# Two paddings in SBUF that shift where the tiles of a convolution and feed-forward kernel begin

## The chip, the cores and the metric

The kernel runs on one core of a Trainium2 chip. The metric is device time in microseconds (us), from three runs of the kernel before: 1163.24, 1163.75 and 1163.84 us, median 1163.75 us. Smaller is better. The engines are named as the profile names them: PE (TensorE's matmuls), PEld (its weight loads), DVE (VectorE), ACT (ScalarE), POOL (GpSimd) and SP (the engine that issues nearly all DMAs).

## The reference

Two layers follow each other. The first is a causal convolution over 7 positions whose weights are given for each token and head, through a softmax; the second is a feed-forward layer with an ELU between its two products.

```python
# x: (4, 4096, 192), weight_gen: (4, 4096, 8 heads, 7 taps)
w = softmax(weight_gen)                       # over the 7 taps
out = einsum('bshk,bskhg->bshg', w, x_unf)    # 7 shifted rows of x, 24 columns per head
# tokens 16384, w_in (192, 2048), w_out (2048, 192)
h = out.reshape(16384, 192) @ w_in
g = where(h > 0, h, exp(min(h, 0)) - 1)       # ELU
return g @ w_out
```

## The kernel before

The 16384 tokens are cut into 32 chunks (`blk`, NB) of 512 tokens, and the 2048 hidden columns into 16 slices (NF), taken two at a time as 8 pairs (`k`, NP). One chunk and one pair make a step `s`: 256 steps. In a step PE forms the two slices' h in PSUM (`product_in`, L685), ACT and DVE make ELU's two parts of them in SBUF (`elu`, L742 to L754), and two steps later PE adds their product with w_out to the sums in PSUM (`product_out`, L713). The convolution of a chunk is made well ahead, nearly all of it on POOL (L508 and L524), and DVE and ACT turn its result into x's parts (`split`, L629 to L639); DMAs on SP's queue then copy parts between the upper and lower 64 partitions (L657).

Precision decides how the operands look. From the second chunk on, each factor is split into a high part, rounded to the type fp32r, and a low part, the rest. So x becomes `xhi` and `xlo`, ELU's value becomes `hi` and `lo` (two rings of seven tiles of 512 columns), w_in becomes `WI` with a high and a low half, and w_out becomes `WO`, whose row holds the high 192 columns and behind them the low 192. h is the sum of three products (xhi with both halves of WI, xlo with the high half) over three pieces of 64 rows: nine matmuls of 512 columns in each half of the partitions. The sum over w_out has a matmul of 384 columns with `hi` as stationary operand (both halves of WO in one go) and one of 192 with `lo`. Only the first chunk (`plain`) uses whole fp32 operands, which take two passes each. Every matmul uses 64 rows of the array, and the upper and lower 64 partitions work side by side: matmuls stand in pairs in the program.

In L685 the stationary operand (loaded on PEld) is a piece of WI and the moving operand is a piece of xhi or xlo. In L713 the stationary operand is a piece of hi or lo, and the moving one a row of WO.

A planner (`Plan`) orders all of it before anything is issued: each task has an engine, a cost from a formula (`pe`, `act`, `dve`, `pool`, `dma`) and a due time, tasks are placed into the earliest gap, and a table (NUDGE) moves some due times. Tiles come from rings (`ring`): the n-th use of a ring waits for the users of the tile that lies `bufs` uses back. No cost, due time or wait depends on an address.

Where a tile lies follows from the order of first use: each tile is placed behind the one before, at a multiple of 32 bytes. The constants come first (`ident`, `scratch`, `WI`, `WO`), then the rings of the pool `sb`. `scratch` is one number per partition, used once to load ACT's table (L885, L886). `wm` holds the largest of the seven weights for each token and head: DVE writes it in L469 and reads it in L471.

Of the kernel before, what the change touches and what calls it, by code (L numbers as in the profile page):

```python
# [10 lines left out]
F32 = mybir.dt.float32  # L11
# [41 lines left out]
class Plan:  # L53
# [13 lines left out]
    def add(self, engine, cost, run, reads=(), writes=(), due=None, port=False):  # L67
        t = Task(engine, cost, run, due, port or engine == "pool")
        for h in reads:
            t.needs.update(h.writers)  # L70
        for h in writes:
            t.needs.update(h.users)
            if not h.users:
                if h.make:
                    t.makes.append(h)
                if h.before:
                    t.needs.update(h.before.users)
        for h in (*reads, *writes):
            h.users.append(t)
        for h in writes:  # L80
            h.writers.append(t)
        t.needs.discard(t)
        t.at = len(self.tasks)
        self.tasks.append(t)
        return t
# [50 lines left out]
def conv_elu_kernel(  # L136
# [12 lines left out]
    P, T, HK = weight_gen.shape  # L149
# [7 lines left out]
    H = HK // K // Q  # L157
# [5 lines left out]
    J = N // (A * S)  # L163
# [38 lines left out]
    def rows(ap, t0, n):  # L202

        return ap.rearrange("(a r) t d -> r a t d", r=R)[t0 // T][:, t0 % T:t0 % T + n]

    def quadrants():

        return [(slice((s * Q + q) * A, (s * Q + q + 1) * A), s, q)
                for s in range(S) for q in range(Q)]

    const = ctx.enter_context(tc.tile_pool(name="const", bufs=1))
# [1 line left out]
    ps = ctx.enter_context(tc.tile_pool(name="ps", bufs=1, space=bass.MemoryType.PSUM))  # L213

    ident = const.tile([P, P], F32, name="ident")
    scratch = const.tile([P, 1], F32, name="scratch")

# [11 lines left out]
    def ring(name, shape, bufs, dtype=F32, pool=sb):  # L231
        return Ring(pool, shape, dtype, name, bufs)
# [4 lines left out]
    r_m_out = ring("m_out", [P, 2, D], 5, I32)  # L237
    r_xw = ring("xw", [P, HALO + J, DQ], 3)
    r_wg = ring("wg", [P, J, H, K], 3)
    r_wm = ring("wm", [P, J, H, 1], 1)  # L240
    r_ws = ring("ws", [P, J, H, 1], 1)
    r_pa = ring("pa", [P, J, H, G], 2)
    r_pb = ring("pb", [P, J, H, G], 1)
# [26 lines left out]
    def act(cols, psum=False):  # L270
        return cols / 1.2 + (70 if psum else 110)

    def dve(cols):
        return cols / 0.96 + 70
# [9 lines left out]
    def dma(packets, byts):  # L284
        return packets * max(9 + byts / 12, 22) / 20
# [7 lines left out]
    def due1(k):  # L293
        if k < len(FIRST):
            return T0 + FIRST[k]
        return T0 + FIRST[-1] + (k - len(FIRST) + 1) * STEP
# [131 lines left out]
    def chunk(blk):  # L428

        n, t0 = J, blk * J * S  # L430
        xw, wg, wm, ws = r_xw.new(), r_wg.new(), r_wm.new(), r_ws.new()
        wg_h[blk] = wg
        xw_h[blk] = xw
        k, kk = n * H, n * H * K

        def w():
            return wg.t[:, 0:n]

        def wide(h):
            return h.t.to_broadcast([P, n, H, K])  # L440

        def load(to, src, n, d, at=0, both=False, only=quadrants()):
            def run():
                for p, s, q in only:
                    eng = nc.scalar if both and q else nc.sync
                    eng.dma_start(out=to()[p], in_=rows(src, t0 + s * J + at, n)[  # L446
                        :, :, q * d:(q + 1) * d])
            return run

        def load_w(only=quadrants()):  # L450
            return load(lambda: w().rearrange("p t h k -> p t (h k)"), weight_gen, n, H * K,
                        both=blk == 0, only=only)

        if blk == 0:
            add("dma", 700 + Q * S * ISSUE // 2, load_w(), writes=[wg], due=-2)
        for one in quadrants() if blk else ():
            add("dma", max(dma(A * n, H * K * 4), ISSUE), load_w([one]), writes=[wg])
        if blk == 0:
            xw_h[blk] = xw = [xw, Handle()]
            m = n + HALO  # L460
            for i, (a, b) in enumerate(((0, m - JH), (m - JH, m))):
                add("dma", dma(P * (b - a), DQ * 4),
                    load(lambda a=a, b=b: xw[0].t[:, a:b], x, b - a, DQ, a),
                    writes=[xw[i]], due=-1 + i)
        else:
            for one in quadrants():
                add("dma", max(dma(A * (n + HALO), DQ * 4), ISSUE),
                    load(lambda: xw.t, x, n + HALO, DQ, only=[one]), writes=[xw])
        add("dve", dve(kk), lambda: nc.vector.tensor_reduce(  # L469
            out=wm.t[:, :, :, 0], in_=w(), axis=AX.X, op=ALU.max), reads=[wg], writes=[wm])  # L470
        add("dve", dve(kk), lambda: nc.vector.tensor_tensor(  # L471
            out=w(), in0=w(), in1=wide(wm), op=ALU.subtract), reads=[wm], writes=[wg], port=True)
        add("act", act(kk), lambda: nc.scalar.activation(
            out=w(), in_=w(), func=ACTF.Exp), writes=[wg])
        add("dve", dve(kk), lambda: nc.vector.tensor_reduce(
            out=ws.t[:, :, :, 0], in_=w(), axis=AX.X, op=ALU.add), reads=[wg], writes=[ws])
        add("act", act(k), lambda: nc.scalar.activation(
            out=ws.t, in_=ws.t, func=ACTF.Copy, bias=1e-9), writes=[ws])
        add("dve", 6.4 * k + 60, lambda: nc.vector.reciprocal(out=ws.t, in_=ws.t),
            writes=[ws])  # L480
        if blk == 0:
            wb_h[blk] = [r_h.new(), r_h.new()]
            for i, h in enumerate(wb_h[blk]):
                def half(t, i=i):
                    return t[:, i * JH:(i + 1) * JH]

                def bank(h=h):
                    return h.t[:, 0:kk // 2].rearrange("p (t h k) -> p t h k", h=H, k=K)

                add("dve", dve(kk // 2), lambda half=half, bank=bank: nc.vector.tensor_tensor(  # L490
                    out=bank(), in0=half(w()), in1=half(wide(ws)), op=ALU.mult),
                    reads=[ws, wg], writes=[h], port=True, due=due1(0) - 14000 + 1000 * i)
                if OWN[blk][i] < K:
                    add("act", act(kk // 2, True), lambda half=half, bank=bank: nc.scalar.copy(
                        out=half(w()), in_=bank()), reads=[h], writes=[wg])
            return
        add("dve", dve(kk), lambda: nc.vector.tensor_tensor(  # L497
            out=w(), in0=w(), in1=wide(ws), op=ALU.mult), reads=[ws], writes=[wg], port=True)
# [384 lines left out]
    with tc.manual_schedule():  # L883

        nc.vector.memset(scratch, 0.0)  # L885
        add("act", 1500, lambda: nc.scalar.activation(out=scratch, in_=scratch, func=ACTF.Exp),  # L886
            due=2500)
        make_identity(nc, ident)
        turn_over(14)
        for s in range(len(todo) + LAG):  # L890
            now = todo[s] if s < len(todo) else None
            up = todo[s - LAG] if s >= LAG else None
            if now:
                blk, k = now
                if k == 0:
                    chunk(blk)
                    if blk < 2:
                        summed(blk, s, OWN[blk])
                    else:
                        conv(blk, s)  # L900
                if blk == 0:
                    if k in in_pieces:
                        weights_in(k, in_pieces[k])
                    weights_out(k)
            period(s, now, up)
            if up and up[1] == NP - 1:
                drain(up[0], s)
        plan.issue()
# [34 lines left out]
```

## Time and profile before

| what | value |
|---|---|
| median of three runs | 1163.75 us |
| runs | 1163.24 to 1163.84 us |
| profiled execution, first to last instruction (span) | 1161.3 us |
| median less span | 2.45 us |
| PE busy | 1154.9 us, 99% of the span |
| PEld, ACT, DVE, POOL busy | 90%, 79%, 73%, 60% |
| share of PE in the chain that ended last | 98% |

The profiled execution has no time of its own beside the span; what lies around it is taken as the difference to the median. Matmuls overlap in the records (a pair starts before the one ahead of it has ended): a busy PE says little, and the distance from one start to the next is what tells the pace.

### The profile page before, as it was taken

To read this page: it belongs to the slowest core of one execution; us is meant where nothing else is said; L and a number is where in the kernel's file an instruction comes from. 1 tells how busy PE (TensorE), PEld (TensorE's weight loads), DVE (VectorE), ACT (ScalarE), POOL (GpSimd) and SP (SyncE) were. 2 spreads that over 40 slices of the span, in tenths; PEclk is the share of its full clock that TensorE was granted. 3 is DMA by queue.
4 is the path that set the end of the run, shared out by engine and by line. 5 is a ranking of instruction groups with operands and counts; after the bars stand their busy time and mean duration, and the time that the engine had idled before them with its cause. 6 is when DMAs were issued, how large, how long until landed. Compare 5 with 4: busy or idle time off the path is not lost.

```text
span 1161.3 us, 32341 instructions
## 1 busy us (share of the span) xinstructions
PE 1154.9 (99%) x12844; PEld 1048.7 (90%) x12844; DVE 847.7 (73%) x1502; ACT 913.7 (79%) x1794; POOL 698.3 (60%) x424
## 2 busy tenths in 40 slices
PE   9999999999999999999999999999999999999998
PEld 6699999999989989989999998998999999999997
DVE  7977768776767777777776677776777776777664
ACT  6778778787778878777878777887777887787775
POOL 4666874846687777865557755567755567653000
PEclk9999999999999999999999999999999999999999
DMA  8831322331233232213332223331223321111100
GB/s 194 165 69 43 65 65 67 71 70 43 57 66 74 49 79 54 59 43 69 70 70 49 47 46 70 71 70 40 53 49 70 70 65 35 26 31 42 42 16 15
DMA packets 143127, 71.04 MB, mean 61 GB/s; under 512 B 98816, under 2 KB 141824, under 8 KB 142976
## 3 DMA queue, kind: packets, MB, share of 16 engines
q1 hardware_dynamic: 142112, 68.72, 27.0%
q8 instruction: 101, 1.65, 0.6%
q14 instruction: 50, 0.41, 0.1%
q10 hardware_dynamic: 864, 0.25, 0.1%
HBM read 31.98 MB, written 12.58 MB: 38 GB/s over the span
## 4 chain that ended last, share of the span: by engine, by line
PE 98%; SPq 1%; DMA 0%; ACT 0%; issue 0%; DVE 0%; DVEq 0%; ACTq 0%
PE h L685 46%; PE accd L713 25%; PE acc L713 25%; PE accd L566 0%; PE acc L566 0%; SPq L446 0%; DMA raw_in<-in_moe_w_in 0%; SPq L369 0%; PE h L681 0%; ACT xhi L646 0%; DVE raw_out L867 0%; ACT acc L329 0%; ACT raw_in L332 0%; SPq L404 0%; ACT raw_out L861 0%
## 5 line engine op out<-in xcount | busy, mean ns | idle before, releaser
L747 DVE SCALAR_TENSOR_TENSOR h<-e,h 128x512 f32<-128x512 f32 x496 | 321.8, 693 | 279.8 <-ACT e L744 278.9
L742 ACT ACTIVATE e<-h 128x512 f32<-128x512 f32 x512 | 280.4, 600 | 171.5 <-PE h L685 171.3
L685 PE MATMUL h<-xhi,WI 64*128 64x512 f32 x2976 | 392.5, 394 | 0.0
L754 DVE TENSOR_TENSOR lo<-h,hi 128x512 fp32r<-128x512 f32 x496 | 326.4, 688 | 14.5 <-ACT hi L752 0.7
L752 ACT CAST hi<-h 128x512 fp32r<-128x512 f32 x496 | 290.7, 587 | 53.9 <-DVE h L747 41.2
L685 PEld LDWEIGHTS h<-xhi,WI 64*128 64x128 f32 x2976 | 279.1, 185 | 48.5
L713 PE MATMUL accd<-WO,hi 64*128 64x384 f32 x1984 | 305.9, 357 | 0.0
L713 PE MATMUL acc<-WO,hi 64*128 64x384 f32 x1984 | 304.6, 355 | 0.0
L524 POOL TENSOR_TENSOR pa<-pa,pb 128x768 f32<-128x768 f32 x150 | 289.9, 1932 | 17.0 <-DVE pb L508 5.5
L744 ACT ACTIVATE e<-e 128x512 f32<-128x512 f32 x512 | 297.9, 637 | 0.9
L508 POOL TENSOR_TENSOR pb<-xw,wg 128x768 f32<-128x768 f32 (+1 forms) x179 | 278.0, 1553 | 11.7
L713 PE MATMUL acc<-WO,lo 64*128 64x192 f32 x1984 | 255.6, 249 | 0.0
L713 PE MATMUL accd<-WO,lo 64*128 64x192 f32 x1984 | 254.8, 248 | 0.0
L508 POOL TENSOR_TENSOR pa<-xw,wg 128x768 f32<-128x768 f32 (+1 forms) x31 | 47.2, 1524 | 305.3 <-DVE wg L497 289.3
L685 PE MATMUL h<-xlo,WI 64*128 64x512 f32 x1488 | 214.6, 390 | 0.0
L713 PEld LDWEIGHTS acc<-WO,lo 64*128 64x128 f32 x1984 | 198.5, 187 | 4.6
L713 PEld LDWEIGHTS acc<-WO,hi 64*128 64x128 f32 x1984 | 196.3, 185 | 4.8
L713 PEld LDWEIGHTS accd<-WO,lo 64*128 64x128 f32 x1984 | 198.8, 188 | 0.1
L713 PEld LDWEIGHTS accd<-WO,hi 64*128 64x128 f32 x1984 | 195.1, 184 | 0.1
L685 PEld LDWEIGHTS h<-xlo,WI 64*128 64x128 f32 x1488 | 144.5, 184 | 28.2
L524 POOL TENSOR_TENSOR xc<-pa,pb 128x768 f32<-128x768 f32 x30 | 55.5, 1851 | 2.4
L639 DVE TENSOR_TENSOR xlo<-xt,xhi 128x768 fp32r<-128x768 f32 (+1 forms) x32 | 37.9, 1184 | 1.0
(84 smaller groups left out, 487.1 us busy)
## 6 DMA issues: line engine op xcount, KB each, us to landing
xw<-in_x SPq DMA_DIRECT2D x124, 168.0 KB, 3.5
xhi<-xhi SPq DMA_DIRECT2D x62, 192.0 KB, 3.0
xlo<-xlo SPq DMA_DIRECT2D x62, 192.0 KB, 2.9
out_dram<-raw_out SPq DMA_DIRECT2D x124, 96.0 KB, 1.9
wg<-in_weight_gen SPq DMA_DIRECT2D x126, 28.0 KB, 2.2
raw_out<-in_moe_w_out SPq DMA_DIRECT2D x8, 384.0 KB, 6.2
raw_in<-in_moe_w_in SPq DMA_DIRECT2D x12, 192.0 KB, 5.3
raw_in<-in_moe_w_in SPq DMA_DIRECT2D x8, 96.0 KB, 2.9
```

Source lines behind the costliest of these rows:

```text
L508: lambda: eng.tensor_tensor(out=h.t[:, 0:J], in0=xw.t[:, j0 + k:j0 + k + J, :].rearrange("p j (h g) -> p j h g", g=G), in1=wg.t[:, j0:j0 + ...
L524: add("pool", pool(J * DQ), lambda b=b, to=to: nc.gpsimd.tensor_tensor(out=to.t, in0=a.t, in1=b.t, op=ALU.add), reads=[b] if to is a else ...
L639: add("dve", dve(C * n * A), lambda i=i: nc.vector.tensor_tensor(out=to(xlo, i), in0=xt(i), in1=to(xhi, i).bitcast(F32), op=ALU.subtract), ...
L685: return lambda: nc.tensor.matmul(out=h.t, lhsT=w_in_f[k][1]()[p, c] if w is None else WI[p, k, w, c], rhs=x.t[p, c, c0:c0 + 2].rearrange( ...
L713: return nc.tensor.matmul(out=to(), lhsT=src.t[p, g * P:(g + 1) * P], rhs=w, start=start, stop=False, skip_group_check=True).ins
L742: add("act", act(N, True), lambda: nc.scalar.activation(out=e.t, in_=h.t, func=ACTF.Relu, scale=-1.0), reads=[h], writes=[e])
L744: add("act", act(N), lambda: nc.scalar.activation(out=e.t, in_=e.t, func=ACTF.Exp, scale=-1.0), writes=[e])
L747: add("dve", dve(N), lambda: nc.vector.scalar_tensor_tensor(out=to.t, in0=e.t, scalar=-1.0, in1=h.t, op0=ALU.add, op1=ALU.max), reads=[e, ...
L752: add("act", act(N, True), lambda: nc.scalar.copy(out=hi.t, in_=h.t), reads=[h], writes=[hi])
L754: add("dve", dve(N), lambda: nc.vector.tensor_tensor(out=lo.t, in0=h.t, in1=hi.t.bitcast(F32), op=ALU.subtract), reads=[h, hi], writes=[lo])
```

## The change

Two tiles that hold few bytes are made larger. `scratch` is allocated with 32 numbers per partition in place of one, and the kernel uses the first; `wm` is allocated with twice its rows, and the kernel uses the first half. Nothing is read or written that was not before, and every engine's instructions and waits stand in the same order with the same shapes.

```diff
-    scratch = const.tile([P, 1], F32, name="scratch")
+    scratch = const.tile([P, 32], F32, name="scratch")[:, 0:1]
...
-    r_wm = ring("wm", [P, J, H, 1], 1)
+    r_wm = ring("wm", [P, 2 * J, H, 1], 1)
...
-        xw, wg, wm, ws = r_xw.new(), r_wg.new(), r_wm.new(), r_ws.new()
+        xw, wg, wm, ws = r_xw.new(), r_wg.new(), r_wm.new(lambda t: t[:, 0:J]), r_ws.new()
```

What moves is the start of each tile behind them. In bytes within a partition (for a ring, its first tile):

```
tile      before   mod 256   mod 64     after    mod 256   mod 64
ident      16512     128        0        16512     128        0
scratch    17024     128        0        17024     128        0
WI         17056     160       32        17152       0        0
WO         41632     160       32        41728       0        0
wg         66208     160       32        66304       0        0
xw         68896      32       32        68992     128        0
wm         85024      32       32        85120     128        0
ws         85152     160       32        85376     128        0
raw_in     85280      32       32        85504       0        0
pa        123680      32       32       123904       0        0
xhi       132896      32       32       133120       0        0
e         160544      32       32       160768       0        0
hi        174368      32       32       174592       0        0
xlo       191776      32       32       192000       0        0
lo        210208      32       32       210432       0        0
xc        224544      32       32       224768       0        0
```

All tiles from WI on began at 32 above a multiple of 64, and begin at a multiple of 64 now. The pieces that a matmul reads lie at multiples of 512 bytes (WI, hi, lo), 1024 (xhi, xlo) or 1536 (WO) from their tile's start, so they share its remainder. WI and WO lay 128 bytes apart from xhi, xlo, hi and lo modulo 256, and lie at the same remainder now.

## Rows read from the trace of the kernel before

**Rows 1.** The page: busy us of each engine, share of the span, instructions.
```profile
PE 1154.9 (99%) x12844; PEld 1048.7 (90%) x12844; DVE 847.7 (73%) x1502; ACT 913.7 (79%) x1794; POOL 698.3 (60%) x424
```

**Rows 2.** The page: chain that ended last, by engine.
```profile
PE 98%; SPq 1%; DMA 0%; ACT 0%; issue 0%; DVE 0%; DVEq 0%; ACTq 0%
```

**Rows 3.** Chain in order of time, steady part: start us, us, what.
```profile
142.29 4.21 PE h L685 x36
151.07 4.21 PE h L685 x36
159.85 4.21 PE h L685 x36
...
1143.39 4.21 PE h L685 x36
```

**Rows 4.** Windows of 8.78 us: busy us of engines, clock, DMA share, GB/s.
```profile
140.00:148.78 8.78, 8.78 (x103) 8.78 (x102) 7.53 (x16) 7.95 (x19) 2.65 (x2) 1.00 0.41 81
148.78:157.56 8.78, 8.78 (x103) 8.78 (x102) 6.71 (x11) 7.23 (x15) 7.99 (x5) 1.00 0.53 125
1000.00:1008.78 8.78, 8.78 (x104) 7.99 (x102) 5.22 (x9) 6.50 (x13) 8.39 (x6) 1.00 0.01 2
```

**Rows 5.** Groups of instructions, PE: shapes, count, busy us, mean ns, idle before.
```profile
L685 PE MATMUL h<-xhi,WI 64*128 64x512 f32 x2976 | 392.5, 394 | 0.0
L713 PE MATMUL accd<-WO,hi 64*128 64x384 f32 x1984 | 305.9, 357 | 0.0
L713 PE MATMUL acc<-WO,hi 64*128 64x384 f32 x1984 | 304.6, 355 | 0.0
L685 PE MATMUL h<-xlo,WI 64*128 64x512 f32 x1488 | 214.6, 390 | 0.0
```

**Rows 6.** Timeline of PE, one step's matmuls and the next stage.
```profile
319.94 1.56 PE L685 MATMUL h<-xhi,WI 64*128 64x512 f32 x12
321.34 0.86 PE L685 MATMUL h<-xlo,WI 64*128 64x512 f32 x6
322.03 0.34 PE L713 MATMUL acc<-WO,hi 64*128 64x384 f32 x2
322.21 0.25 PE L713 MATMUL acc<-WO,lo 64*128 64x192 f32 x2
322.30 0.36 PE L713 MATMUL acc<-WO,hi 64*128 64x384 f32 x2
322.50 0.25 PE L713 MATMUL acc<-WO,lo 64*128 64x192 f32 x2
322.58 0.37 PE L713 MATMUL acc<-WO,hi 64*128 64x384 f32 x2
```

**Rows 7.** Timeline of PEld in the same stage.
```profile
322.21 0.19 PEld L713 LDWEIGHTS acc<-WO,hi 64*128 64x128 f32 x2
322.32 0.19 PEld L713 LDWEIGHTS acc<-WO,lo 64*128 64x128 f32 x2
322.50 0.19 PEld L713 LDWEIGHTS acc<-WO,hi 64*128 64x128 f32 x2
```

**Rows 8.** Chain in the first chunk, with whole fp32 operands.
```profile
32.10 2.58 PE h L685 x12
34.68 0.16 PE accd L713
```

**Rows 9.** Weight loads of two lines: duration ns min/median/max, first and last start.
```profile
L566 PEld LDWEIGHTS acc<-v,ident x28: 186/190/190, 7.3 to 39.9; 128*128 128x128 f32 x28
...
L685 PEld LDWEIGHTS h<-xhi,WI x2976: 183/185/189, 61.0 to 1146.3; 64*128 64x128 f32 x199
```

**Rows 10.** Chain in the prologue: start us, us, what.
```profile
9.41 3.78 DMA raw_in<-in_moe_w_in
13.18 0.02 issue
...
15.49 2.98 PE h L681 x24
```

**Rows 11.** The same DMAs, issue to landing.
```profile
DMA to landing us min/median/max: 2.3/4.4/7.5
```

**Rows 12.** POOL's additions of the convolution: duration ns min/median/max.
```profile
L524 POOL TENSOR_TENSOR pa<-pa,pb x150: 1820/1852/2670, 58.2 to 1048.5; 128x768 f32<-128x768 f32 x150
```

## The prediction

> **What bounds the kernel now.** I read the busy line first: PE is busy for 99% of the span, ACT for 79%, DVE for 73% [rows 1]. A busy PE alone proves little, so the second view is the chain that ended last: 98% of it is PE's own work, with 1% of SP's issue at the start [rows 2]. The third is that chain in order of time. The reader is to see how regular it is: from 142.29 us to 1143.39 us the same stretch of 36 matmuls of L685 returns, and 1001.10 us are 114 times 8.78 us to within 0.2 us [rows 3]. The fourth is a table of windows of just that length. In three of them POOL's work goes from 2.65 to 8.39 us, DVE's from 7.53 to 5.22 and the share of the DMA engines from 0.53 to 0.01, at a granted clock of 1.00 (2.4 GHz) [rows 4], and the period stays 8.78 us. So PE waits for nobody there, and nobody's traffic in SBUF slows it. What the change can do to the time is what it does to PE's own reading of its operands, and next to nothing else.
>
> The pace inside a period: nine pairs of matmuls of 512 columns, from 319.94 to 322.03 us, are 2.09 us, or 232 ns a pair [rows 6]. In L713 one round of `hi` (384 columns) and `lo` (192) takes from 322.30 to 322.58, 0.28 to 0.29 us, 288 ns when the period is divided: (8.78 - 18 x 0.232) / 16 [rows 3, 6]. Counts: 2976 + 1488 matmuls of L685 are 2232 pairs, and 1984 + 1984 of `hi` are 1984 rounds [rows 5]. 2232 x 0.232 = 518 us and 1984 x 0.288 = 571 us: 1089 of the 1161.3 us, and the rest is prologue, first chunk and the last sums.
>
> **The change part by part.** It adds, removes and moves no instruction, wait or DMA on any queue. It alters start addresses, so each term is the difference in how long the same instruction takes.
>
> 1. *L685's matmuls.* 512 columns at one per cycle of 2.4 GHz would be 213 ns; a pair takes 232, 19 more. The trace has one neighbour: with whole fp32 operands in the first chunk 12 matmuls, six pairs, take 2.58 us, 430 ns a pair [rows 8], which is two cycles per column (426.7) and 3 ns. xhi began 32 bytes above a multiple of 64 there as well. So a shifted start costs nothing when a column has two cycles, and 16 ns remain that show only at one column per cycle. Nothing in this trace says whether these 16 ns come from the start address or belong to reading 4 bytes per cycle: no operand of that kind begins elsewhere. Bounds: below, all 16 ns go, 2232 x 0.0156 = 35 us less; above, a collision of the two operands, which the third case prices at as much again, 35 us more. Value taken: 0, as for the nearest row, the fp32 pass, where the same start costs nothing that can be seen.
>
> 2. *L713's rounds.* The loads for `lo` start 0.11 us after those for `hi`, and the matmuls with `lo` start 0.18 us after that, with which the next loads for `hi` start [rows 7, 6]: a round is one load of 128 columns and one stream of 384. The load can be compared: L566 loads `ident`, which begins at a multiple of 128 in both kernels, in 190 ns, and L685 loads WI, shifted by 32, in 185 [rows 9]. The start does not lengthen a load, so that part gets 0. The stream of 384 takes 0.18 us against 160 ns at 2.4 GHz. Of the 20 ns, 3 are again the fixed part; 10 to 17 could go or double: 20 to 33 us either way over 1984 rounds. Value taken: 0, for the reason of point 1.
>
> 3. *ACT, DVE and POOL.* They too read and write at new starts. Whatever it does to them stands beside PE's stream: ACT, the fullest, works 7.95 of 8.78 us in the fullest of the three windows [rows 4], so it would have to become 10% slower before PE waits. 0.
>
> 4. *DMAs.* The only one in the chain is w_in's load, 3.78 us of it, before PE's first product at 15.49 us [rows 10]. Landings of its kind lie between 2.3 and 7.5 us [rows 11], so -1.5 to +3.7 us are the bounds; the bytes and the source rows in HBM are as before, and I take 0. All later DMAs have PE's period as cover.
>
> The sum against the profiled execution is 1161.3 + 0, and with the 2.45 us around it 1163.7 us.
>
> Here the Trainium skill speaks against a gain: SBUF — State Buffer, Specifications (TRN2), gives lines of 16 bytes and a penalty for each step to a new line. Every start was a multiple of 32 already, so by that rule no operand touches one line more or less, and the sum stays 1163.7; the equal weight loads agree, and no row shows the lines themselves.
>
> **The rivals.**
>
> *The shift is what costs PE its 16 ns (faster).* For it: the excess appears only where a column has a single cycle, it grows with the columns (19 ns on 512, while from `lo`'s start to the next `hi`, over 192 columns, it is 0.08 to 0.09 us against 80 ns [rows 6]), and all operands of this kind share the one odd start. A stall for each block of 64 bytes would look like this. Against it: a contiguous stream that starts shifted touches 33 blocks of 64 bytes in place of 32, which is 3% at most, not 7%; and loads don't mind. Price: L685 gives 35 us and L713 at least 20, together 55: 1109 us. If only half of the excess is due to the start, 1136. ACT's 7.95 us would then stand against a period of some 8.4, so not every block would gain in full.
>
> The Trainium skill has a figure for this rival: TensorE: Matmul & The Clock Gate, Back-to-back issue gap, gives N/2.4 + 2.5 ns between matmuls, 215.7 ns for 512 columns. By it 16 ns of 232 are no part of the stream, and without them in L685 alone the time would be 1128 us as an estimate; the fp32 rows agree with such a fixed part (3 ns), and the page doesn't tie it to an address.
>
> *Both of PE's reads fall in step (slower).* WI and WO lay 128 bytes apart from the operands that they meet, modulo 256, and now lie at the same remainder. If PE's weight load and its stream meet in the same part of SBUF, they wait for each other during each load, 0.11 of every 232 ns. For it: two engines can slow each other here, as POOL's additions do, with 1852 ns in the median and 2670 at worst [rows 12]. Against it: the two read at different speeds, so their phase slides through all remainders anyway, and no other reader ever disturbed PE's 8.78 us [rows 3, 4]. It decides from about 1 ns a pair (2.3 us over 2232 pairs). Price: one more excess of the present size in L685, 35 us, 1199 us; at POOL's worst ratio, 44% on each load's 0.11 us, it would be 48 ns a pair and 1271.
>
> *The prologue alone moves.* w_in's first load lands earlier or later within its bounds: 1162.2 to 1167.4 us. The first is within what can be told from no change (2.3 us, 0.2%), the second is just beyond.
>
> **How the numbers follow.** No change: 0.50, and its own range is 1161.4 to 1166.1. The shift costs PE its excess: 0.37, with times from 1109 to 1160. In step: 0.11. The prologue by itself beyond 0.2%: 0.02, slower. About 0.2% is what a measurement of this kernel can tell from no change. So faster 0.37, same 0.50, slower 0.13. The range goes from 1108, the full price of the faster rival, to 1167.4, the prologue's worst: outside lie the slower rival and a gain beyond 55 us, together under 2 in 10.
>
> **What would show it.** If I am right, the period stays 8.78 us, nine pairs 2.09 us and a round 288 ns, and the span differs by under 2 us, at the start. If nine pairs take 1.94 to 2.0 us, the faster rival holds for L685, and a shorter step from `hi` to `lo` shows it for L713. If only L685 or only L713 becomes longer, the reads are in step there. A changed period with unchanged distances inside the two stages would mean a wait that I have not seen, and all of this would be wrong.

## The result, and the profile after

1150.81 us in the median of 4 runs (1150.17 to 1152.1), against 1163.8 us of before beside it: ratio 0.9891, 95% interval 0.9877 to 0.9905. The kernel became 1.1% faster. The time lies inside the forecast range; the likeliest case, no change, did not come about, and the period, forecast to stay at 8.78 us, became 8.67.

The page of the kernel after: busy time of each engine, and the chain that ended last by engine.
```profile
PE 1141.7 (99%) x12844; PEld 1039.1 (90%) x12844; DVE 852.0 (74%) x1502; ACT 912.2 (79%) x1794; POOL 697.9 (61%) x424
...
PE 96%; SPq 1%; ACT 1%; DVE 1%; issue 0%; DMA 0%; DVEq 0%; ACTq 0%
```
PE is still busy for 99% and still holds the chain, now 96% of it where it had 98% [rows 1, 2]. The span is 1149.1 us, 12.2 less than in the profiled execution of before.

The chain of the kernel after, in order of time: start us, us, what.
```profile
306.63 4.15 PE h L685 x36
310.77 1.11 PE acc L713 x16
311.89 1.14 PE accd L713 x16
313.02 1.14 PE acc L713 x16
314.16 1.14 PE accd L713 x16
315.30 4.15 PE h L685 x36
...
323.97 4.15 PE h L685 x36
...
349.99 4.15 PE h L685 x36
```
The period was 8.78 us [rows 3]; it is (349.99 - 306.63) / 5 = 8.67 us now, with nobody but PE in it. PE does the same 36 + 64 matmuls in 0.11 us less.

The timeline of PE in the same kernel, one whole period: start us, us, instruction.
```profile
332.48 1.57 PE L685 MATMUL h<-xhi,WI 64*128 64x512 f32 x12
333.89 0.86 PE L685 MATMUL h<-xlo,WI 64*128 64x512 f32 x6
334.59 1.53 PE L685 MATMUL h<-xhi,WI 64*128 64x512 f32 x12
335.95 0.84 PE L685 MATMUL h<-xlo,WI 64*128 64x512 f32 x6
336.63 0.34 PE L713 MATMUL acc<-WO,hi 64*128 64x384 f32 x2
336.80 0.25 PE L713 MATMUL acc<-WO,lo 64*128 64x192 f32 x2
336.89 0.36 PE L713 MATMUL acc<-WO,hi 64*128 64x384 f32 x2
...
341.16 1.57 PE L685 MATMUL h<-xhi,WI 64*128 64x512 f32 x12
```
The second nine pairs take 336.63 - 334.59 = 2.04 us; before they took 2.09 [rows 6]. Sixteen rounds of L713 take 341.16 - 336.63 = 4.53 us. Medians over all steady periods (from start to start of the matmul records, between 150 and 1120 us): the block of L685, its 18 pairs, went from 4206 to 4147 ns, and that of L713, its 16 rounds, from 4574 to 4526. That is 3.3 ns a pair and 3.0 ns a round. Over 124 periods (2232 pairs / 18) it is 7.3 + 6.0 = 13.3 us, more than the 12.2 that the span lost.

The two profiled executions differ in two more places. First, in the prologue of the kernel after (chain):
```profile
9.90 3.70 DMA raw_in<-in_moe_w_in
...
15.96 2.98 PE h L681 x24
18.94 2.58 PE h L685 x12
```
The first product starts 0.47 us later than in [rows 10], and the fp32 pairs take the same 2.58 us as in [rows 8]. Second, in waits. The chain of the kernel after around 666 us:
```profile
664.57 0.33 SPq L876
...
666.38 1.80 SPq L446
...
668.75 0.02 SPq L700
...
668.81 1.39 PE acc L713 x16
```
PE reaches this L713 while SP's queue still issues DMAs (L876, L446), behind which stands the no-op of L700 that L713 waits for. This period lasts 9.11 us. After has three periods more than 60 ns too long, by 0.96 us together; before had two, by 0.26. So 13.3 - 0.5 - 0.7 = 12.1 us, the span's loss to within 0.1. Neither difference is shown to come from the change. Over all the runs below the first product starts between 15.42 and 16.28 us, and e1, e2 and e3, whose pace is nearly that of before, have 0.87 to 1.08 us of such long periods, with waits for L700 as well (in e3 three, 0.8 us together).

The weight loads, duration ns min/median/max:
```profile
L713 PEld LDWEIGHTS accd<-WO,hi x1984: 183/184/185, 76.1 to 1144.1; 64*128 64x128 f32 x199
```
A load's own record is as long as L685's in [rows 9]; only the step from one instruction to the next became shorter.

### The profile page after: what moved, and what is told of

It is laid out like the page before. It is cut to its first block, busy times and chain, and to the rows that moved or that the text cites. A ratio compares the mean times of both kernels' runs of the same rounds, so it can differ in the third digit from the quotient of the medians.

```text
span 1149.1 us, 32341 instructions
## 1 busy us (share of the span) xinstructions
PE 1141.7 (99%) x12844; PEld 1039.1 (90%) x12844; DVE 852.0 (74%) x1502; ACT 912.2 (79%) x1794; POOL 697.9 (61%) x424
## 4 chain that ended last, share of the span: by engine, by line
PE 96%; SPq 1%; ACT 1%; DVE 1%; issue 0%; DMA 0%; DVEq 0%; ACTq 0%
PE h L685 45%; PE accd L713 25%; PE acc L713 24%; SPq L446 1%; PE accd L566 0%; PE acc L566 0%; SPq L876 0%; DMA raw_in<-in_moe_w_in 0%; ACT hi L752 0%; SPq L369 0%; ACT e L742 0%; PE h L681 0%; DVE h L747 0%; DVE raw_out L867 0%; ACT e L744 0%
## 5 line engine op out<-in xcount | busy, mean ns | idle before, releaser
L685 PE MATMUL h<-xhi,WI 64*128 64x512 f32 x2976 | 388.1, 390 | 0.0
L685 PEld LDWEIGHTS h<-xhi,WI 64*128 64x128 f32 x2976 | 277.9, 185 | 46.9
L713 PE MATMUL accd<-WO,hi 64*128 64x384 f32 x1984 | 306.1, 356 | 0.0
L713 PE MATMUL acc<-WO,hi 64*128 64x384 f32 x1984 | 303.1, 353 | 0.3 <-SPq L700 0.2
L713 PE MATMUL accd<-WO,lo 64*128 64x192 f32 x1984 | 256.4, 247 | 0.0
L713 PE MATMUL acc<-WO,lo 64*128 64x192 f32 x1984 | 256.3, 247 | 0.0
L685 PE MATMUL h<-xlo,WI 64*128 64x512 f32 x1488 | 214.7, 389 | 0.0
L713 PEld LDWEIGHTS acc<-WO,lo 64*128 64x128 f32 x1984 | 198.6, 187 | 4.2
L713 PEld LDWEIGHTS acc<-WO,hi 64*128 64x128 f32 x1984 | 196.3, 184 | 5.1 <-SPq L700 0.8
L713 PEld LDWEIGHTS accd<-WO,lo 64*128 64x128 f32 x1984 | 199.0, 188 | 0.0
L713 PEld LDWEIGHTS accd<-WO,hi 64*128 64x128 f32 x1984 | 195.8, 184 | 0.0
L685 PEld LDWEIGHTS h<-xlo,WI 64*128 64x128 f32 x1488 | 145.2, 185 | 27.2
L639 DVE TENSOR_TENSOR xlo<-xt,xhi 128x768 fp32r<-128x768 f32 (+1 forms) x32 | 41.7, 1304 | 1.0
```

The lines of the kernel that those rows point to most:

```text
L639: add("dve", dve(C * n * A), lambda i=i: nc.vector.tensor_tensor(out=to(xlo, i), in0=xt(i), in1=to(xhi, i).bitcast(F32), op=ALU.subtract), ...
L685: return lambda: nc.tensor.matmul(out=h.t, lhsT=w_in_f[k][1]()[p, c] if w is None else WI[p, k, w, c], rhs=x.t[p, c, c0:c0 + 2].rearrange( ...
L713: return nc.tensor.matmul(out=to(), lhsT=src.t[p, g * P:(g + 1) * P], rhs=w, start=start, stop=False, skip_group_check=True).ins
```

## The experiments

Three theories are tested in the runs below. S: the moving operand (x's parts, WO) stalls PE when it begins inside a block of 64 bytes. W: the stationary one (WI, `hi`, `lo`) does. P: neither start counts, but the distance between the two, modulo 256: 128 bytes before, 0 after. A fourth, O, is named in the expectation of e1: that the tiles of other engines count. "Distance" below is stationary minus moving, modulo 256; "blocks" are the medians of L685's 18 pairs and of L713's 16 rounds in ns, worked out as above. "Measured" gives the ratio to the runs of before beside it, with its 95% interval.

**e1_moving**: only the moving operands at multiples of 64.
```diff
-    WO = const.tile([P, NF, 2 * D], F32R, name="WO")
+    WO = const.tile([P, NF * 2 * D + 16], F32R, name="WO")[:, 8:8 + NF * 2 * D].rearrange("p (f m) -> p f m", f=NF)
-    r_xhi = ring("xhi", [P, C, 3, NS], 2, F32R)
+    r_xhi = ring("xhi", [P, C * 3 * NS + 16], 2, F32R)
...
+        xhi = r_xhi.new(shifted, dtype=F32 if blk == 0 else None)
```
(xlo likewise; `shifted` is the view from element 8 on.)

> Only the moving operands (xhi, xlo, WO) begin at a multiple of 64 bytes; WI, hi, lo and all other tiles stay at 32 above one. Theory S (the stream pays for a shifted start): the whole gain, about 1151 us, period 8.67 us, 18 pairs of L685 4.15 us and 16 rounds of L713 4.53 us. Theory W (the weight load pays): no gain, 1163.8 us, period 8.78 us. Theory P (what counts is how the two operands lie to each other modulo 256 bytes): both distances change to 160 or 192 here, so anything but the value after. Theory O (other engines' tiles count): no gain.

Measured: 0.9993 (0.9984 to 1.0001), blocks 4210 and 4562. No gain: S falls. By the sizes of the tiles the distances here are 32 and 224 for xhi, 96 and 160 for xlo (its ring and that of xhi have two tiles each), 32 for `hi` and 160 for `lo`: none is 0, so P allows this too.

**e2_stationary**: only the stationary operands at multiples of 64.
```diff
+    WI = const.tile([P, NP * 2 * C * P + 16], F32R, name="WI")[:, 8:8 + NP * 2 * C * P].rearrange("p (k i c m) -> p k i c m", k=NP, i=2, c=C)
...
+    r_hi = ring("hi", [P, N + 16], 7, F32R)
...
+            hi, lo = (r.new(lambda t: t[:, 8:8 + N]) for r in (r_hi, r_lo))
```
(`r_lo` likewise.)

> Only the stationary operands (WI, hi, lo) begin at a multiple of 64 bytes; xhi, xlo, WO and all others stay at 32 above one. Theory S: no gain, 1163.8 us, period 8.78 us. Theory W: the whole gain, about 1151 us, with the gain in L713's rounds, where a load stands in the chain. Should both operands count, e1 and e2 share the 13 us between them.

Measured: 1.0007 (0.9998 to 1.0016), blocks 4218 and 4568. W falls. The distances are 96 and 160 in L685, and 32, 96, 160 or 224 in L713, where each of the seven tiles of a ring lies 64 bytes further than the one before: again none is 0.

**e3_off32**: a first padding of 16 elements puts every tile at a multiple of 64; the distances stay 128.
```diff
+    scratch = const.tile([P, 16], F32, name="scratch")[:, 0:1]
```

> scratch of 16 numbers: every tile behind it moves by just 32 bytes, to 64 above a multiple of 128 (WI and WO at 192 modulo 256, the rest at 64), 128 bytes apart as before. Theories S and W (a block of 64 bytes is the unit): as after, 1151 us, period 8.67 us. If the unit is 128 or 256 bytes: no gain or part of it. Theory P (same distance as before): 1163.8 us.

Measured: 0.9999 (0.999 to 1.0008). The chain of this run:
```profile
336.31 4.30 PE h L685 x36
...
345.09 4.30 PE h L685 x36
```
The period is 8.78 us, as before. (A piece of the chain ends where the next matmul hands over, so 4.30 beside 4.21 is another cut; the blocks are 4206 and 4574, before's to the nanosecond.) With S and W together, all operands at multiples of 64, alignment without a new distance does nothing.

**e4_wm_only**: the change's second padding alone. All starts stay 32 bytes above a multiple of 64, the distances become 0.
```diff
-    r_wm = ring("wm", [P, J, H, 1], 1)
+    r_wm = ring("wm", [P, 2 * J, H, 1], 1)
...
+        xw, wg, wm, ws = r_xw.new(), r_wg.new(), r_wm.new(lambda t: t[:, 0:J]), r_ws.new()
```

> Only the second padding (wm): all operands stay at 32 above a multiple of 64 (160 modulo 256), but WI and WO now lie at the same remainder modulo 256 as xhi, xlo, hi and lo. Theories S and W: 1163.8 us, period 8.78 us. Theory P: as after, 1151 us; if reads in step collide, slower.

Measured: 0.989 (0.9875 to 0.9905). Its chain:
```profile
333.03 4.15 PE h L685 x36
...
341.70 4.15 PE h L685 x36
```
8.67 us, blocks 4147 and 4526: all of the gain, at starts that are no multiple of 64, let alone of 256. P is left, and O is decided by e5 and e11. What the change does for the time it does by the distance of two operands, not by where the tiles begin.

**e5_wi_only**: distance 0 for WI and x, 128 for `hi` and WO (the kernel before with this edit alone; WO's longer tile moves the rings by 128 bytes).
```diff
+    WO = const.tile([P, NF * 2 * D + 32], F32R, name="WO")[:, 32:32 + NF * 2 * D].rearrange("p (f m) -> p f m", f=NF)
```

> WO begins 128 bytes later within its tile, and the rings behind it lie 128 bytes further: WI meets xhi and xlo at distance 0 modulo 256, WO still meets hi and lo at 128; all starts stay at 32 above a multiple of 64. Theory P (distance between a matmul's own two operands): L685's block takes 4147 ns as after, L713's 4574 ns as before, about 1157 us. If it is a distance between other tiles (the rings against w_generator's or x's window tiles, or DVE's and POOL's operands), both stages change together: 1151 or 1164 us.

Measured: 0.9921 (0.9906 to 0.9936). Its chain:
```profile
334.00 4.12 PE h L685 x36
338.12 1.14 PE acc L713 x16
...
342.70 4.12 PE h L685 x36
```
L685 is short (4126), L713 as long as before (4574), period 8.70 us. Each stage goes by its own two operands, and O, by which both would have changed together, falls. L685 is 21 ns shorter than in after, where 4147 was expected: at the same distance its block differs a little with the stage ahead of it, and no run shows how.

**e6_d64**, **e7_d192**, **e8_d512**: other paddings of `wm`, for the shape and the modulus (with `scratch` as in before, like e4).
```diff
+    r_wm = ring("wm", [P, J + n, H, 1], 1)    # n = 12, 4 and 24
```

> wm with 12 more rows: distance 64 modulo 256 between WI, WO and the operands that they meet. Theory P with one bad distance (128): as after, 1151 us. With one good distance (0): as before, 1164 us. With a cost that grows with the distance: in between, about 1157 us.

> wm with 4 more rows: distance 192 modulo 256 (64 bytes before the start of the other operand's block). One bad distance: 1151 us; one good distance: 1164 us; a cost that depends on which operand leads: different from the run at distance 64.

> wm with 24 more rows: distance 0 modulo 512, where after has 0 modulo 256 but 256 modulo 512. If 256 bytes is the period: as after, 1151 us, L685 4147 and L713 4526 ns. If the period is 512 or more: another time, as before (1164 us) or better than after.

Measured: e6 0.9937 (0.9921 to 0.9954), e7 0.998 (0.997 to 0.9989), e8 0.9885 (0.9871 to 0.99). By distance:
```
distance        0      64      128     192
L685         4147    4227     4206    4157
L713         4526    4563     4574    4533
```
The operands of L685 and L713 lie in opposite order, so that one run has 64 in one stage and 192 in the other: e6 has 192 in L685 and 64 in L713, e7 the reverse. Neither expectation held, one bad distance or one good one: in L685, 192 is nearly as good as 0, and 64 is worse than 128. e8, whose distance is 0 modulo 512 too, has the same blocks as after: 256 does it.

**e9_lead224**, **e10_lead32**: both stages at 224, and both at 32 (`scratch` as in before).
```diff
+    WO = const.tile([P, NF * 2 * D + 16], F32R, name="WO")[:, 16:16 + NF * 2 * D].rearrange("p (f m) -> p f m", f=NF)
+    r_wm = ring("wm", [P, J + 6, H, 1], 1)    # e10: 48 and J + 10
```

> Distances are now given as stationary operand less moving operand, modulo 256. So far, L685's block / L713's: at 0 4147 / 4526 ns, at 64 4227 / 4563, at 128 4206 / 4574, at 192 4157 / 4533. Here both are 224 (WI 32 bytes before xhi and xlo, hi and lo 32 bytes before WO). If 0 is the best place and the cost rises smoothly from it: about 4152 / 4530 and 1152.5 us. If 0 is one point of a flat or lower stretch between 192 and 0: 4147 / 4526 or less, 1151 us or less. If what counts is equality of the start alone: as at 192 or worse, 1153 us and up.

> Both distances 32: the stationary operand starts 32 bytes behind the moving one's remainder. The load goes at half the stream's pace and starts with it, so a stream that begins behind the load's place catches up with it. If that meeting is what costs: nearly as bad as 64 (4227 / 4563), about 1161 us. If the cost rises smoothly with distance from 0: half way, 4187 / 4545, about 1157 us.

Measured: 1.0 (0.9991 to 1.001), blocks 4215 and 4565; 1.0003 (0.9993 to 1.0013), blocks 4221 and 4566. Neither side of 0 is nearly as good as 0. The cost is no smooth function of the distance, and the expectations of one failed; what came was, in e9, the third of its cases, and in e10 a block nearly as bad as at 64. The reason that e10's expectation gives for it, a stream that catches up with its load, is not shown by this.

**e11_micro**: the kernel after, with 32 groups of matmuls added at its end. Most groups are 12 pairs of 512 columns at one distance; the additional products go nowhere. No other engine works beside them.
```diff
+        for at, (ds, m, halves) in enumerate(sets):
+            for n in range(12):
...
+                    w = 1024 + n % 2 * 128 + ds[n % len(ds)] // 4
+                    nc.tensor.matmul(out=outs[at % 2][i][0:m, 0:cols], lhsT=wf[p, w:w + m], rhs=xf[p, 1, c0:c0 + 2].rearrange("p s n -> p (s n)")[:, 0:cols], start=True, stop=True, skip_group_check=True)
```

> The kernel after, with 32 groups of 12 matmul pairs appended behind its last sums (some 85 us of extra work, whose results nobody uses). Each group has one shape and one distance (stationary start less moving start, modulo 256; the moving operand is xhi, the stationary one is read from WI). Theory P: pairs of 512 columns take 227 ns at distance 0 and 230 to 236 at 64 and 128; at 32 and 224 234 or so, and at other multiples of 16 no better than 227. If the weight load that runs beside a stream is what the distance acts on: in the group that alternates 0 and 128, the stream beside which the weights at 128 are loaded is the slow one, not the stream that uses them; with loads of 32 columns a pair takes less than with 128, at both distances, near 216 ns if all of the excess is due to the load. If the distance acts through something else, loads of 32 columns change nothing and the pair with its own distance 128 is the slow one. With one half of the partitions alone: the same times, if the two halves don't disturb each other.

Measured in a single execution. The timeline of PE, groups at distance 0, 16, 32, ..., 128, 144, ..., 192, 208, ..., and then loads of 32 columns at 0 and at 128, of 64 at 128:
```profile
1148.07 2.88 PE L919 MATMUL acc<-xhi,WI 64*128 64x512 f32 x24
1150.79 2.89 PE L919 MATMUL h<-xhi,WI 64*128 64x512 f32 x24
1153.52 2.95 PE L919 MATMUL acc<-xhi,WI 64*128 64x512 f32 x24
...
1170.29 2.96 PE L919 MATMUL acc<-xhi,WI 64*128 64x512 f32 x24
1173.09 2.96 PE L919 MATMUL h<-xhi,WI 64*128 64x512 f32 x24
...
1181.44 2.91 PE L919 MATMUL acc<-xhi,WI 64*128 64x512 f32 x24
1184.19 2.96 PE L919 MATMUL h<-xhi,WI 64*128 64x512 f32 x24
...
1203.63 2.94 PE L919 MATMUL acc<-xhi,WI 64*32 64x512 f32 x24
1206.41 2.92 PE L919 MATMUL h<-xhi,WI 64*32 64x512 f32 x24
1209.17 2.92 PE L919 MATMUL acc<-xhi,WI 64*64 64x512 f32 x24
```
From start to start, by 12: 2.72 us or 227 ns a pair at 0, 2.73 or 227 at 16, 2.80 or 233 at 128, 2.75 or 229 at 192. From the single records without a group's first two pairs: 226.7 ns at 0 and 16, 227.0 at 240, 228.9 at 192, 229.9 at 176, and 232 to 234 at 32 to 160, 208 and 224. At distances of 4, 8 and 24 bytes it is 232.4, 230.8 and 230.0. DVE, ACT and POOL are idle from 1148 to 1226 us, so the distance acts on PE without any other engine. With loads of 32 columns it is 231 at both distances: there the distance made no difference, and the 216 ns that the expectation gave, had the load made the whole excess, did not come. With a single half of PE at work it is 229 falling to 227 at 0, and 232 at 128: the halves don't need each other for it. Four groups that alternate 384 and 192 columns, as L713 does, are too short to settle: a round takes 287 ns at 128 and has come down to 282 in the last round at 0. A group that alternated between 0 and 128 gave 232 without a pattern, so it is not settled which of the two counts for a stream, its own weights or those loaded beside it.

**e12_wi16**: the kernel after with WI 16 bytes further, since 16 did as well as 0 in e11.
```diff
+    WI = const.tile([P, NP * 2 * C * P + 64], F32R, name="WI")[:, 4:4 + NP * 2 * C * P].rearrange("p (k i c m) -> p k i c m", k=NP, i=2, c=C)
```

> The kernel after, with WI 16 bytes further: distance 16 in L685, 0 in L713 as in after. In the appended groups 512-column pairs took 226.7 ns from the first at distance 16 and at 0. In after, the first nine of L685's 18 pairs take up to 236 ns before they fall to 227. If those nine are an effect of how load and stream start against each other, distance 16 may let them fall at once: L685's block 4110 ns, about 1146 us. If they come from the passage out of L713 alone: 4147 and 1151 us. If 16 holds only where the pairs before were already at 226.7: 4200 or so, 1158 us.

Measured: 0.9929 (0.9916 to 0.9943), slower than after. Its chain at two places:
```profile
684.35 4.27 PE h L685 x36
693.11 4.27 PE h L685 x36
...
711.23 4.11 PE h L685 x36
719.86 4.11 PE h L685 x36
```
The same instructions at the same distances have two paces, blocks of 4222 and of 4107 to 4114 ns, and nothing between. One pace holds over many periods (49 blocks of 4222 from 281 to 701 us, then 50 of the short kind up to 1135), and here it changes where PE waited for SP's queue once, just before 711 us. Two earlier changes in the steady part, at 220 us to the short blocks and at 281 us back, also follow on an L713 stage that was 0.14 to 0.17 us too long, while other long stages changed nothing. So something besides the distance sets the pace; that it is how the loads and streams stand to each other after such an interruption is likely, but not shown. No version that was run beats the kernel after; e4 and e8 equal it within their intervals. A version that held the pace of 4108 from the start was not tried.

## Why the prediction was right or wrong, point by point

**The range held by luck.** 1150.81 us lies in it because it reaches down to 1108, the full price of a rival whose cause the runs refute. By its own signs (a period of 8.78 us, nine pairs in 2.09 us, a round of 288 ns) the forecast of no change failed: the step that failed is the value 0 of points 1 and 2, where the measured terms are -7.3 and -6.0 us.

**What bounds the kernel: right.** The gain is in PE's pace and nowhere else, and where PE's operands lie is the only thing that changed there.

**Point 1, "Value taken: 0": wrong by 7.3 us.** The sum had the nearest row for it, the fp32 pass, where the start costs nothing. That row was read rightly and answers another question: it shows a start, and e3 and e4 show that the start is not what counts. The distance, which does count, had no term in this sum; it stood only among the rivals. Measured: -3.3 ns a pair, nearly all of it in the second nine pairs of a block (2.09 to 2.04 us; the first nine lose about 9 ns).

**Point 2, "that part gets 0": wrong by 6.0 us.** The equal loads of [rows 9] were right, and they stayed equal. But a round is the step from one load and stream to the next, and equal records do not make an equal step: -3.0 ns a round.

**The rule of the Trainium skill** (SBUF — State Buffer, Specifications (TRN2): a penalty at each new line of 16 bytes) was weighed for no change. By it no operand touches a line more or less, in e4 either, and e4 gained 12.9 us. So the rule does not reach what acted here, and the measurement decides against it as a reason for no change.

**The faster rival: the right side, the wrong cause.** A shifted start costs PE nothing: e1, e2 and e3 lie within 0.1% of 1. Of its 16 ns a pair 3.3 went, 5 once the pairs run at 226.7, and its test, nine pairs in 1.94 to 2.0 us, was not met (2.04). The Trainium skill's gap (TensorE: Matmul & The Clock Gate, Back-to-back issue gap), 215.7 ns for 512 columns, which the page gives for a matmul by itself, is not reached by the one-pass pairs of any run: 226.7 was the best of a settled group.

**"Both of PE's reads fall in step": the right quantity with the wrong sign.** This rival named what the runs showed to be the cause, the distance modulo 256 going from 128 to 0, and priced it as a collision, +35 us. It is a gain of 13.3. No row that the prediction shows gave the sign: [rows 12] shows that POOL's additions differ in length, not what lengthened them. Its argument against itself, that "their phase slides through all remainders anyway", did not hold either: if the distances evened out, the pace could not depend on them, and e11 has 226.7 ns at 0 and 233.8 at 128. That PE's pace depends on how its two operands lie to each other is shown by e4, e5 and e11; that load and stream meet in reading SBUF is only likely.

**Points 3 and 4: right in the time.** The prologue of the profiled execution was 0.47 us longer, inside its bounds and within the scatter of the runs. DVE's subtraction for xlo became slower (L639's median from 1227 to 1451 ns), beside PE's stream; e4 has this too (1484) and e3 does not (1233), so it does not come from the starts. The threshold was right as well: some ns a pair are enough to show. The waits for SP's queue had no step in the prediction, which took all later DMAs as covered; they come and go with the execution by some 0.7 us, in runs with the pace of before too.

**Open:** why 227 ns and not 213; why the first pairs after L713 run slower than the later ones; what sets the pace that e12 keeps; and what in PE the distance acts on.

## What to carry to other kernels

When PE's own stream is the bound, try the stationary and the moving operand of the hot matmuls at the same remainder modulo 256, by a padding anywhere between their tiles, and look at the pace of single pairs afterwards; it was shown here for one kernel, with fp32r operands on 64 rows. Price a change of addresses by pairs of operands that are read at once, not by the starts alone: each start of e4 was as odd as before, and it had the whole gain. If a quantity changes that can act either way and no row shows its sign, price both signs and give each a chance; a new distance can also do nothing (e1, e2, e9 and e10 lie within 0.1% of 1).

## What the runs showed of the hardware

- In settled pairs of one-pass fp32r matmuls on 64 rows, 512 columns take 226.7 ns at best (e11), at a granted clock of 1.00. That is 17/16 of 512 columns at 2.4 GHz (213.3 x 17/16 = 226.7); no run shows why.
- The distance of the operands modulo 256 moves this by up to 7.7 ns a pair (e11: 226.7 at 0, 233.8 at 128, 234.4 at 96), and not evenly: 16 and 240 are as good as 0 in a settled run, 32 and 224 are as bad as 128, and 4, 8 and 24 lie between (230.0 to 232.4).
- The same program at the same distances can keep either of two paces for hundreds of us (e12: 4222 or 4113 ns a block).
